# Folding the sinks into the preceding block's rows, with three displaced keys added back by VectorE

## The chip, the cores and the metric

One Trainium2 chip, of which the kernel uses one core. The metric is the device time of one execution in microseconds (us). Executions agree within about 1%; where a run was marked as disturbed (one execution each of two experiments) it is left out of the ratios. The profile is one execution on the same core. A result or run below gives a ratio with its 95% interval; differences under 2% are clear of noise only where that interval leaves out 1. The engines are TensorE (PE), VectorE (DVE), ScalarE (ACT), GpSimd (POOL) and SyncE (SP); SP here only issues DMAs, and GpSimd issues the loads.

## The reference, cut to what matters

```python
# q, k, v: (4, 8, 768, 64) float32; n_sink = 4; window = 128
scores = matmul(q, k.T) / sqrt(64)
keep = (pos < n_sink) | ((rel >= 0) & (rel < window))     # rel = query - key
a = softmax(where(keep, scores, -1e9));  x = matmul(a, v)  # -> (4, 768, 512)
xn = (x - mean) / sqrt(var + 1e-6) * g_ln
out = x + relu(xn @ w_ch1) @ w_ch2                        # 512 -> 2048 -> 512
```

Each query sees the first four keys of its batch (the sinks) and the last 128 keys.

## The kernel before: the parts that matter

There are 24 blocks of 128 queries: block `t` is block `r = t % 6` of batch `b = t // 6`. A block with `r > 0` multiplies its queries with the keys of its own and of the preceding block; from `r = 2` on the sinks are in neither, and get small products of their own. Four blocks make a group, which goes through the two layers of the MLP (`ph` and `pc` in the profile). All instructions come from a planner: a task has a cost, dependencies and a priority, and the planner writes each engine's instructions in the order of its simulated starts. The tiles that matmuls write have names in p: `ps` and `pk` scores, `pv` and `po` products with the values, `pt` and `px` transposes. Fillers are matmuls against the identity, put where the planner expects PE to wait.

```python
def load(fn, land, take=(), desc=1024):               # all q, k, v and weight loads, on GpSimd
    i = plan.add({"POOL": 0.88}, [], fn, (0,), take=take, land=land, after=last_load[0], desc=desc)
...
# sc(): scores of the own and the preceding block go to ps; then, for r >= 2, the sinks' scores:
for h2 in range(2):
    for hp in range(4):
        nc.tensor.matmul(P["pk", t][32 * hp:32 * hp + 32, h2, :], lhsT=ks_of[b][:, h2, hp, :],
                         rhs=qkT[t][:, 0, hp, :], ...)
...
# ACT: exponentials of ps and, apart, of pk (es). av(), for each half of the heads:
if r >= 2:
    for h2 in range(2):
        nc.tensor.matmul(po..., lhsT=ES[t][:, h2, :], rhs=vs_t[b]..., start=(h2 == 0), ...)
for hh in range(4):
    nc.tensor.matmul(po[:, hh, :], lhsT=ee[...0, :], rhs=vn[:, t, h, :], ...)
    if r > 0:
        nc.tensor.matmul(po[:, hh, :], lhsT=ee[...1, :], rhs=vn[:, t - 1, h, :], ...)
...
# from block 8 or so on SP transposes queries and keys by DMA; it also stores the output
nc.sync.dma_start_transpose(qkT[t]..., qn[t]...)
```

What matters of the planner: a dependency fixes a *position in the order of an engine's instructions*. At run time an instruction waits only for data and buffers it really needs.

The softmax here doesn't subtract the row's maximum and nothing guards it: scores larger than these inputs give would overflow.

## Time and profile before

227.5 us, median of 3 runs (227.4 to 227.82).

| | before |
|---|---|
| span of the profiled run | 225.4 us |
| PE busy | 217.0 us (96%) |
| DVE / ACT busy | 135.0 / 104.0 us |
| DMA full until | about 130 us |

PE is the bound, except in the first 26 us, where loads are. The prediction below shows the lines. The first DMA transposes start here (columns: start, length in us, the instruction):

```profile
51.82 5.67 SPq L369 DMA_TRANSPOSE qkT<-qkn  x2
```

### The profile page before, as it was taken

What the parts mean: (1) busy time and instruction counts of PE and PEld (TensorE: products, weight loads), DVE (VectorE), ACT (ScalarE), POOL (GpSimd) and SP (SyncE); (2) the same over time, 40 slices, a digit from 0 to 9 for tenths busy, and PEclk for the clock granted to TensorE, in tenths of its full rate; (3) what the DMA queues carried; (4) which work ended last, traced back from release to release, by engine and by line L of the source; (5) the groups of instructions that cost most, each with busy time, mean ns of one, the idle gap of its engine ahead of it and who ended that gap; (6) DMA issues with size and microseconds to landing.
All of it is one profiled execution on the core that took longest, in us unless ns stands there. A gap on an engine that the chain in (4) does not pass through costs nothing.

```text
span 225.4 us, 4783 instructions
## 1 busy us (share of the span) xinstructions
PE 217.0 (96%) x1921; PEld 121.0 (54%) x1948; DVE 135.0 (60%) x398; ACT 104.0 (46%) x166; POOL 76.0 (34%) x92
## 2 busy tenths in 40 slices
PE   8999999999999999999999999999999999999992
PEld 7766787655455554455555544454555544444440
DVE  5777998779577988863756873654854712100121
ACT  2386788344367731167641258633077600376000
POOL 7994366691695242933088000100000010000000
PEclk9999999999999999999999999999999999999999
DMA  7999999999999999999989994203221021200111
GB/s 43 139 157 206 182 184 209 166 173 192 218 150 129 144 140 189 175 185 191 94 103 158 168 209 88 51 17 102 71 48 23 3 70 47 93 0 3 47 71 69
DMA packets 108709, 26.52 MB, mean 118 GB/s; under 512 B 101520, under 2 KB 105616, under 8 KB 108688
## 3 DMA queue, kind: packets, MB, share of 16 engines
q0 software_dynamic: 79104, 13.64, 81.7%
q1 hardware_dynamic: 29584, 12.59, 30.1%
q8 instruction: 15, 0.25, 0.4%
q14 instruction: 6, 0.05, 0.1%
HBM read 27.27 MB, written 6.29 MB: 149 GB/s over the span
## 4 chain that ended last, share of the span: by engine, by line
PE 81%; DMA 8%; POOL 5%; DVE 3%; issue 1%; ACT 0%; POOLq 0%; ACTq 0%
PE ph L603 34%; PE pc L634 34%; PE ps L406 5%; DMA w1s<-in_moe_w_ch_dram 4%; DMA qkT<-qkn 3%; PE po L501 2%; PE po L504 2%; POOL qkn L267 2%; POOL vn L275 2%; POOL qkn L272 2%; PE po L496 2%; PE pk L413 1%; PE pt L347 1%; DVE xt L517 1%; DVE w1s L299 1%
## 5 line engine op out<-in xcount | busy, mean ns | idle before, releaser
L603 PE MATMUL ph<-xnt,w1s 128*128 128x512 bf16 (+1 forms) x434 | 88.9, 348 | 1.0 <-DVE h L617 0.3
L634 PE MATMUL pc<-w2s,h 128*128 128x512 bf16 x371 | 87.0, 379 | 1.1 <-issue 0.5
L619 ACT ACTIVATE h<-ph 128x512 bf16<-128x512 f32 (+1 forms) x84 | 45.8, 546 | 53.8 <-PE ph L603 52.1
L603 PEld LDWEIGHTS <-w1s 128*128 128x128 bf16 x448 | 41.5, 98 | 35.4 <-ACT h L619 0.5
L634 PEld LDWEIGHTS <-h 128*128 128x128 bf16 x384 | 35.8, 98 | 39.1
L435 ACT ACTIVATE e<-ps 128x1024 bf16<-128x1024 f32 (+1 forms) x48 | 43.7, 951 | 12.5 <-PE ps L406 12.5
L646 DVE SCALAR_TENSOR_TENSOR ot<-pc,rsg,xt 128x512 f32<-128x512 f32 x24 | 17.9, 747 | 38.9 <-PE pc L634 38.9
L548 POOL TENSOR_TENSOR rsg<-ve,eps_half 128x4 f32<-128x4 f32 x6 | 6.2, 1028 | 82.0 <-DVE ve L546 82.0
L267 POOL DMA_DIRECT2D qkn<-in_q_dram x24 | 21.9, 910 | 14.9 <-DMA qkT<-qkn 13.1
L444 DVE TENSOR_TENSOR e<-e,mask_std 128x1024 bf16<-128x1024 bf16 x28 | 18.9, 684 | 10.9 <-ACT e L435 10.9
L617 DVE TENSOR_SCALAR h<-ph 128x512 bf16<-128x512 f32 (+1 forms) x28 | 15.9, 570 | 13.7 <-PE ph L603 13.6
L272 POOL DMA_DIRECT2D qkn<-in_k_dram x24 | 21.7, 903 | 2.8 <-DMA w2s<-in_moe_w_ch_dram 1.4
L275 POOL DMA_DIRECT2D vn<-in_v_dram x24 | 21.8, 912 | 1.8 <-DMA w1s<-in_moe_w_ch_dram 1.8
L517 DVE SCALAR_TENSOR_TENSOR xt<-po,rc 128x256 bf16<-128x256 f32 x48 | 20.4, 425 | 1.7
L501 PE MATMUL po<-vn,e 128*128 128x65 bf16 x192 | 17.1, 193 | 0.1
L537 DVE BATCH_NORM_STATS2 st<-xt 128x6 f32<-128x512 bf16 x24 | 16.4, 684 | 0.0
L406 PEld LDWEIGHTS <-qkT 64*128 64x128 bf16 x352 | 9.9, 94 | 10.4 <-issue 7.8
L406 PE MATMUL ps<-qkT 64*128 64x128 bf16 x352 | 14.7, 218 | 0.7 <-DMA qkT<-qkn 0.4
L482 ACT ACTIVATE es<-pk 128x256 bf16<-128x256 f32 x16 | 6.1, 383 | 19.9 <-PE pk L413 19.8
L514 DVE RECIPROCAL rc<-po 128x4 f32<-128x4 f32 x48 | 8.5, 178 | 11.3 <-PE po L504 10.4
L501 PEld LDWEIGHTS <-e 128*128 128x128 bf16 x192 | 14.0, 97 | 2.1 <-DVE e L444 0.5
L504 PE MATMUL po<-vn,e 128*128 128x65 bf16 x160 | 14.9, 193 | 0.0
(66 smaller groups left out, 146.2 us busy)
## 6 DMA issues: line engine op xcount, KB each, us to landing
out_dram<-ot SPq DMA_DIRECT2D x24, 256.0 KB, 2.5
qkn<-in_q_dram POOLq DMA_DIRECT2D x24, 128.0 KB, 7.1
qkn<-in_k_dram POOLq DMA_DIRECT2D x24, 128.0 KB, 6.8
vn<-in_v_dram POOLq DMA_DIRECT2D x24, 128.0 KB, 7.6
w1s<-in_moe_w_ch_dram POOLq DMA_DIRECT2D x4, 512.0 KB, 10.3
w2s<-in_moe_w_ch_dram POOLq DMA_DIRECT2D x4, 512.0 KB, 10.7
qkT<-qkn SPq DMA_TRANSPOSE x16, 7.2
xnt<-xc SPq DMA_TRANSPOSE x16, 5.6
```

What stands on the lines that cost most here:

```text
L267: nc.gpsimd.dma_start(qn[t][:, 0], q[b, :, rows, :].rearrange("h p d -> p h d"))
L272: nc.gpsimd.dma_start(qn[t][:, 1], k[b, :, rows, :].rearrange("h p d -> p h d"))
L275: nc.gpsimd.dma_start(vn[:, t, :, 0:64], v[b, :, rows, :].rearrange("h p d -> p h d"))
L406: nc.tensor.matmul(ps[:, h2, hh, kb, :], lhsT=qkT[t - kb][rows, 1, hp, :], rhs=qkT[t][rows, 0, hp, :], start=(hh == 0 and kb == 0 and t no ...
L435: nc.scalar.activation(E[t, half][:, :, :, 0:nkb, :], P["ps", t, half][:, :, :, 0:nkb, :], AF.Exp, scale=scale)
L444: nc.vector.tensor_mul(ee[:, :, 0:w], ee[:, :, 0:w], m[:, 0:w].unsqueeze(1).to_broadcast([128, 4, w]))
L501: nc.tensor.matmul(po[:, hh, :], lhsT=ee[:, h % 2, hh // 2, 0, :], rhs=vn[:, t, h, :], start=(r < 2 and hh == 0), stop=(r == 0), skip_grou ...
L504: nc.tensor.matmul(po[:, hh, :], lhsT=ee[:, h % 2, hh // 2, 1, :], rhs=vn[:, t - 1, h, :], start=False, stop=True, skip_group_check=True)
L517: nc.vector.scalar_tensor_tensor(xt[t][:, 256 * half:256 * half + 256].rearrange("p (h d) -> p h d", h=4), in0=po[:, :, 0:64], scalar=1.0, ...
L603: nc.tensor.matmul(ph, lhsT=w1s[:, j, 128 * ht:128 * (ht + 1)], rhs=xnt[g][:, j, cols], start=(j == 0), stop=(j == NDM - 1))
L619: nc.scalar.activation(o, i, AF.Relu)
L634: nc.tensor.matmul(P["pc", t], lhsT=h1[g, ht][:, 128 * ti:128 * (ti + 1)], rhs=w2s[:, ht, :], start=(ht == 0), stop=(ht == NH1 - 1))
```

## The change

The intent: for the eight blocks with `r >= 2` of batches 2 and 3 (14 to 17 and 20 to 23) copy the four sinks over rows 0 to 3 of the preceding block's keys and values. Queries 3 and up of a block do not see those rows anyway, so the sinks need no products of their own. Queries 0, 1 and 2 lose up to three keys that they should see (rows 1 to 3 of the preceding block). Their contribution is computed apart in float32 by DVE, and added to rows 0 to 2 of the result. The inputs of that are fetched by 27 small DMAs. In the same change the planner's model of DMA landing times is altered, two buffer rings shrink, and the variance may run on ACT.

```diff
+    def corrections(dep):
+        for i in range(3):
+            def fetch(e, i=i):
+                for b in range(1, B):
+                    at = slice(12 * i + 4 * (b - 1), 12 * i + 4 * b)          # four partitions
+                    nc.sync.dma_start(fq[at], q[b, :, 256:768, :].rearrange("h (r x) d -> x r h d", x=128)[i])
+                    for to, src in ((fk, k), (fv, v)):
+                        nc.sync.dma_start(to[at].rearrange("r h p d -> r h (p d)"),
+                                          src[b, :, 129:641, :].rearrange("h (r x) d -> r h x d", x=128)[:, :, 0:3, :]
+                                          .rearrange("r h x d -> r h (x d)"))
+            fetched.append(plan.add({"SP": 4.0}, [dep], fetch, (0, 7, i), land=.7, lag=2.0, ...))
         ... fourteen DVE operations on 36 partitions, one ACT exponential -> fc ...
+        def spread(e):
+            for i in range(3):
+                nc.sync.dma_start(fcb[i:i + 1], fc[12 * i:12 * i + 12])
 ... in block(t), with fold = r >= 2 and t >= FOLD (12):
+        if fold:
+            nc.vector.tensor_copy(qkT[t - 1][:, 1, :, 0:4], kss_of[b])        # sinks' keys
+            nc.vector.tensor_copy(vn[0:4, t - 1], vn[0:4, t - r])             # sinks' values
-        sink = r >= 2 and halves[-1] == 1
+        sink = r >= 2 and not fold and halves[-1] == 1
-                if r >= 2:
+                if sinks:                                                     # r >= 2 and not fold
                     ... the sinks' products in po ...
+                if fold:
+                    nc.vector.tensor_add(po[0:3], po[0:3], fcb[:, t - RB - 2 * b, 4 * half:4 * half + 4, :])
 ... and elsewhere:
-    RINGS = dict(... ks=2, vs=2, ... xn=4, h1=32, ot=4)
+    RINGS = dict(... ks=2, kss=2, vs=2, ... xn=2, h1=20, ot=4)
-        v_ = d_var[t] = plan.add({"DVE": .87}, ...)
+        v_ = d_var[t] = plan.add({"DVE": .87, "ACT": .95}, ...)               # ACT: Square with accum_out
+    corrections(quanta[FDEP])                                                 # FDEP = 32, a piece of the MLP
 ... cut: the planner's landing(), a lag for each load, masks, counts of readers
```

More of the change, by code (lines that the diff above doesn't have):

```diff
@@ L47, in run @@
         ends = {}
-        dma_free = free["DMA"]
+        dma = {"POOL": free["DMA"], "SP": free["DMA"]}
         order = []
@@ L94, in run @@
             if t["land"] is not None:
-                dma_free = max(dma_free, start + 1.5) + t["land"]
-                end = dma_free + (0.6 if t["lag"] is None else t["lag"])
+                at = self.landing(dma, e, start, t["land"])
+                end = at + (0.6 if t["lag"] is None else t["lag"])
                 if t["desc"]:
-                    queued.append((dma_free, t["desc"]))
+                    queued.append((at, t["desc"]))
             done[i] = (e if t["land"] is None else None, start + cost, end)
@@ L112, in run, with landing @@
         return order
+    @staticmethod
+    def landing(dma, e, start, land):
+        if e == "POOL":
+            dma["POOL"] = max(dma["POOL"], start + 1.5) + land
+        else:
+            begin = max(dma["SP"], start + 1.5)
+            dma["SP"] = begin + land + min(land, max(0.0, dma["POOL"] - begin))
+            dma["POOL"] = max(dma["POOL"], begin) + land
+        return dma[e]
     @staticmethod
@@ L165 @@
     LDN, QKN = 4, 5
-    RINGS = dict(pa=4, ps=2, ld=LDN, qk=QKN, ks=2, vs=2, e=8, es=3, xc=4, xn=4, h1=32, ot=4)
+    RINGS = dict(pa=4, ps=2, ld=LDN, qk=QKN, ks=2, kss=2, vs=2, e=8, es=3, xc=4, xn=2, h1=20, ot=4)
     plan = Planner(RINGS)
@@ L206 @@
     ks_t = [consts.tile([128, 2, 4, 32], BF16, name=f"ks_{i}") for i in range(2)]
+    junk = consts.tile([128, DM], BF16, name="junk")
+    kss = [consts.tile([128, 4, 4], BF16, name=f"kss_{i}") for i in range(2)]
+    mask_c = consts.tile([36, 1, 3], FP32, name="mask_c")
+    tmp_c = consts.tile([36, 1, 3], FP32, name="tmp_c")
+    iota_c = consts.tile([36, 3], I32, name="iota_c")
+    fq = consts.tile([36, H, 64], FP32, name="fq")
+    fk = consts.tile([36, H, 3, 64], FP32, name="fk")
+    fv = consts.tile([36, H, 3, 64], FP32, name="fv")
+    fs = consts.tile([36, H, 3], FP32, name="fs")
+    fe = consts.tile([36, H, 3], FP32, name="fe")
+    fc = consts.tile([36, H, 65], FP32, name="fc")
+    fcb = consts.tile([3, 12, H, 65], FP32, name="fcb")
     xt = [consts.tile([128, DM], BF16, name=f"xt_{t}") for t in range(NT)]
@@ L221, in make_masks @@
         nc.gpsimd.iota(iota_h, pattern=[[-32, 4]], base=0, channel_multiplier=1)
+        nc.gpsimd.iota(iota_c, pattern=[[12, 3]], base=12, channel_multiplier=-1)
         v_.tensor_scalar(ident, iota_d, 0.0, None, op0=ALU.is_equal)
@@ L251 @@
     last_load = [None]
+    n_load = [0]
     def load(fn, land, take=(), desc=1024):
-        i = plan.add({"POOL": 0.88}, [], fn, (0,), take=take, land=land, after=last_load[0], desc=desc)
+        n = n_load[0]
+        n_load[0] += 1
+        i = plan.add({"POOL": 1.4 if n == 0 else 0.9}, [], fn, (0,), take=take, land=land, after=last_load[0], desc=desc,
+                     lag=.9 if n < 8 else 2.4 if n < 42 else 1.2)
         last_load[0] = i
@@ L313 @@
     P = {}
+    folds = []
     def w0(e, s):
@@ L324, in opening, with mask, step @@
         D["mc"] = plan.add({"DVE": 1.3}, [d_q[0]], make_masks_c, (0, 1, 5))
+    def corrections(dep):
+        fetched = []
+        for i in range(3):
[7 more added lines that the diff above has]
+                                          .rearrange("r h x d -> r h (x d)"))
+            fetched.append(plan.add({"SP": 4.0}, [dep], fetch, (0, 7, i), land=.7, lag=2.0,
+                                    after=fetched[-1] if fetched else None))
+        def mask(e):
+            nc.vector.tensor_scalar(mask_c[:, 0, :], iota_c, 0.0, None, op0=ALU.is_gt)
+        def step(cost, deps, fn, eng="DVE"):
+            return plan.add({eng: cost}, deps, fn, (0, 7, 8))
+        d = step(.2, fetched, mask)
+        for p in range(3):
+            d = step(.65, [d], lambda e, p=p: nc.vector.tensor_mul(fk[:, :, p, :], fk[:, :, p, :], fq))
+            d = step(.65, [d], lambda e, p=p: nc.vector.tensor_reduce(
+                fs[:, :, p:p + 1], fk[:, :, p:p + 1, :], axis=mybir.AxisListType.X, op=ALU.add))
+        d = step(.3, [d], lambda e: nc.scalar.activation(fe, fs, AF.Exp, scale=scale), "ACT")
+        d = step(.2, [d], lambda e: nc.vector.tensor_mul(fe, fe, mask_c.to_broadcast([36, H, 3])))
+        for p in range(3):
+            d = step(.65, [d], lambda e, p=p: nc.vector.tensor_mul(
+                fv[:, :, p, :], fv[:, :, p, :], fe[:, :, p:p + 1].to_broadcast([36, H, 64])))
+        d = step(.2, [d], lambda e: nc.vector.tensor_reduce(fc[:, :, 64:65], fe.unsqueeze(2),
+                                                            axis=mybir.AxisListType.X, op=ALU.add))
+        d = step(.65, [d], lambda e: nc.vector.tensor_add(fv[:, :, 0, :], fv[:, :, 0, :], fv[:, :, 1, :]))
+        d = step(.65, [d], lambda e: nc.vector.tensor_add(fc[:, :, 0:64], fv[:, :, 0, :], fv[:, :, 2, :]))
+        def spread(e):
+            for i in range(3):
+                nc.sync.dma_start(fcb[i:i + 1], fc[12 * i:12 * i + 12])
+        done = plan.add({"SP": 1.4}, [d], spread, (0, 7, 9), land=.2, lag=2.0)
+        for i in folds:
+            plan.tasks[i]["deps"].append(done)
@@ L335, in block @@
         split = t in SPLIT
+        fold = r >= 2 and t >= FOLD
         def tr(a):
@@ L356, in block @@
         n_s = lambda u: 2 if u in SPLIT_S else 1
-        qk_readers = n_s(t) + (0 if last else n_s(t + 1)) + (1 if r == 0 else 0)
+        qk_readers = n_s(t) + (0 if last else n_s(t + 1)) + (sum(any((u >= FOLD) == w for u in range(t + 2, t + RB)) for w in (0, 1)) if r == 0 else 0)
         if split:
@@ L416, in sc, with fold_k, fold_v @@
             return f
+        if fold:
+            def fold_k(e):
+                nc.vector.tensor_copy(qkT[t - 1][:, 1, :, 0:4], kss_of[b])
+            def fold_v(e):
+                nc.vector.tensor_copy(vn[0:4, t - 1], vn[0:4, t - r])
+            kf = plan.add({"DVE": .13}, [d_s[t - 1], d_kss[b]], fold_k, (0, t, 1), drop=[("kss", b)])
+            vf = plan.add({"DVE": .25}, d_a[t - 1] + [d_v[t - r]], fold_v, (0, t, 1))
         s_ = []
@@ L420, in block @@
             cost = .22 * nkb + .43 * nkb * (t in MPE)
-            sink = r >= 2 and halves[-1] == 1
+            sink = r >= 2 and not fold and halves[-1] == 1
             x_ = plan.add({"PE": cost * len(halves) / 2 + .15 + SINK * sink},
                           d_c[t] + (d_c[t - 1] if r else []) + ([D["mb"]] if t in MPE and r else [])
-                          + ([d_ks[b]] if sink else []), sc(halves),
+                          + ([d_ks[b]] if sink else []) + ([kf] if fold else []), sc(halves),
                           (0, t, 2), take=[("ps", ("ps", t, h), 1) for h in halves]
@@ L440, in mk @@
             def mk(e, half=half):
-                m = (mask_zero, mask_one)[r] if r < 2 else mask_std
+                m = mask_zero if r == 0 else mask_one if r == 1 or fold else mask_std
                 w = 128 * nkb
@@ L446, in block, with mkf @@
             ms.append(x_ if t in MPE else plan.add({"DVE": .68 if r else .4}, [x_], mk, (0, t, 4)))
-        if r == 0:
+        blocks = [u for u in range(t + 2, t + RB)] if r == 0 else []
+        old = [u for u in blocks if u < FOLD]
+        new = [u for u in blocks if u >= FOLD]
+        if new:
+            def mkf(e, s):
+                kss_of[b] = kss[s]
+                nc.vector.tensor_copy(kss[s], qkT[t][:, 1, :, 0:4])
+            d_kss[b] = plan.add({"DVE": .13}, d_c[t], mkf, (0, t + 2, 0), take=[("kss", ("kss", b), len(new))],
+                                drop=[("qk", t)])
+        if old:
             def mks(e, s):
@@ L454, in mks @@
                     nc.vector.tensor_copy(ks_of[b][rows, h2], qkT[t][rows, 1, :, 0:32])
-            d_ks[b] = plan.add({"DVE": .3}, d_c[t], mks, (0, t + 2, 0), take=[("ks", ("ks", b), 4)],
+            d_ks[b] = plan.add({"DVE": .3}, d_c[t], mks, (0, t + 2, 0), take=[("ks", ("ks", b), len(old))],
                                drop=[("qk", t)])
@@ L468, in block @@
                 pv = plan.add({"PE": .13}, [d_v[t], D["mc"], s_[0]] + vs_d, pv_, (0, t + 2, 0),
-                              take=[("pa", ("pv", b, half), 1)] + ([("vs", ("vs", b), 8)] if half == 0 else []))
+                              take=[("pa", ("pv", b, half), 1)] + ([("vs", ("vs", b), 2 * len(old))] if half == 0 else []))
                 def vs_(e, half=half, hs=hs):
@@ L477, in block @@
             d_vs[b] = vs_d
-        a_deps = [d_v[t]] + ([d_v[t - 1]] if r else [])
-        if r >= 2:
+        a_deps = [d_v[t]] + ([d_v[t - 1]] if r else []) + ([vf] if fold else [])
+        sinks = r >= 2 and not fold
+        if sinks:
             def es_(e):
@@ L493, in av @@
                 ee = E[t, half]
-                if r >= 2:
+                if sinks:
                     for h2 in range(2):
@@ L501, in av @@
                     nc.tensor.matmul(po[:, hh, :], lhsT=ee[:, h % 2, hh // 2, 0, :], rhs=vn[:, t, h, :],
-                                     start=(r < 2 and hh == 0), stop=(r == 0), skip_group_check=True)
+                                     start=(not sinks and hh == 0), stop=(r == 0), skip_group_check=True)
                     if r > 0:
@@ L505, in av @@
                                          start=False, stop=True, skip_group_check=True)
-            a = plan.add({"PE": (.12, .25, .37)[min(r, 2)]}, a_deps + [ms[half]], av, (0, t, 5),
+            a = plan.add({"PE": .12 if r == 0 else .37 if sinks else .25}, a_deps + [ms[half]], av, (0, t, 5),
                          take=[("pa", ("po", t, half), 1)],
-                         drop=[("e", t, half)] + ([("es", t), ("vs", b)] if r >= 2 else []))
+                         drop=[("e", t, half)] + ([("es", t), ("vs", b)] if sinks else []))
+            d_a.setdefault(t, []).append(a)
             def nm(e, half=half):
                 po = P["po", t, half]
+                if fold:
+                    nc.vector.tensor_add(po[0:3], po[0:3], fcb[:, t - RB - 2 * b, 4 * half:4 * half + 4, :])
                 rc = small.tile([128, 4], FP32, name="rc")
@@ L520, in nm @@
                     accum_out=sums[t][:, half:half + 1])
-            ns.append(plan.add({"DVE": .60}, [a], nm, (0, t, 6), drop=[("po", t, half)]))
+            if fold:
+                folds.append(len(plan.tasks))
+            ns.append(plan.add({"DVE": .93 if fold else .60}, [a], nm, (0, t, 6), drop=[("po", t, half)]))
         def ln(e, s):
@@ L535, in st @@
                 mvg[g] = small.tile([128, 4, 2], FP32, name="mvg")
-            st_ = small.tile([128, 6], FP32, name="st")
-            nc.vector.bn_stats(st_, xt[t])
-            nc.vector.bn_aggr(mvg[g][:, ti, :], st_)
-        v_ = d_var[t] = plan.add({"DVE": .87}, [l_] + ([d_var[t - 1]] if ti else []), st, (0, t + 6, 7))
+            if e == "DVE":
+                st_ = small.tile([128, 6], FP32, name="st")
+                nc.vector.bn_stats(st_, xt[t])
+                nc.vector.bn_aggr(mvg[g][:, ti, :], st_)
+            else:
+                root = 1.0 / float(DM) ** 0.5
+                st_ = small.tile([128, 1], FP32, name="nb")
+                nc.scalar.mul(st_, sums[t][:, 2:3], -root)
+                nc.scalar.activation(junk, xt[t], AF.Square, bias=st_, scale=root, accum_out=mvg[g][:, ti, 1:2])
+        v_ = d_var[t] = plan.add({"DVE": .87, "ACT": .95}, [l_] + ([d_var[t - 1]] if ti else []), st, (0, t + 6, 7))
         if ti == len(GROUPS[g]) - 1:
@@ L582 @@
     quanta = []
-    ks_of = {}
+    ks_of, kss_of, d_kss, d_a = {}, {}, {}, {}
     h1 = {}
@@ L668 @@
     W2AT = 6
+    FOLD = 12
+    FDEP = 32
     SEQ = [x for g in range(NG) for x in ((1, g), (2, g))]
```

## The prediction

> **What bounds the kernel now.** I read the page first, then the busy time of each engine by stretch, then TensorE's timeline around one late attention block, then the chain of waits in the opening. One core, so there is no die to compare, and the granted clock is full.
>
> The page: busy time, the chain that ended last by engine, and the DMA row of the 40 slices.
>
> ```profile
> PE 217.0 (96%) x1921; PEld 121.0 (54%) x1948; DVE 135.0 (60%) x398; ACT 104.0 (46%) x166; POOL 76.0 (34%) x92
> ...
> DMA  7999999999999999999989994203221021200111
> ...
> PE 81%; DMA 8%; POOL 5%; DVE 3%; issue 1%; ACT 0%; POOLq 0%; ACTq 0%
> ```
>
> TensorE (PE) carries four fifths of the chain. What is not PE is DMA and GpSimd's issuing of loads, and the DMA row says when: the engines are full from the first slices to about 130 us and nearly empty after it.
>
> Busy time in four stretches (columns: PE, its weight loads, DVE, ACT, GpSimd; then clock, DMA share, GB/s):
>
> ```profile
> 0.00:27.00 27.00, 25.27 (x339) 19.31 (x340) 20.16 (x77) 15.43 (x24) 20.18 (x29) 1.00 1.53 145
> 27.00:60.00 33.00, 32.25 (x353) 21.95 (x355) 27.78 (x82) 18.07 (x34) 18.75 (x22) 1.00 1.87 180
> 60.00:180.00 120.00, 118.44 (x1054) 61.28 (x1069) 80.68 (x231) 60.45 (x92) 36.04 (x41) 1.00 1.20 120
> 180.00:222.00 42.00, 41.05 (x188) 18.48 (x189) 6.34 (x11) 10.01 (x17) 1.01 (x1) 1.00 0.13 47
> ```
>
> From 60 us on PE is busy 118.4 of 120 us while DVE is at two thirds and ACT at half: PE work removed there should come off the end one for one. The first stretch differs: part of PE's 25.3 busy us are warming matmuls against the identity that the schedule puts where it expects PE to wait. After the 34 on zeros there are 66 of them (the rows of that one line count 37 + 13 + 11 + 5), about 56 ns apart.
>
> One late block, from PE's timeline (start, length, then the instruction):
>
> ```profile
> 163.60 0.62 PE L406 MATMUL ps<-qkT 64*128 64x128 bf16 x16
> 164.15 0.29 PE L413 MATMUL pk<-qkT,ks 128*32 128x128 bf16 x8
> 164.38 2.76 PE L603 MATMUL ph<-xnt,w1s 128*128 128x512 bf16 x11
> 166.98 0.28 PE L496 MATMUL po<-vs,es 128*128 128x130 bf16 x2
> 167.10 0.19 PE L501 MATMUL po<-vn,e 128*128 128x65 bf16 x1
> ```
>
> Read starts, not lengths, because matmuls overlap: the eight sink scores (pk) occupy PE from 164.15 to 164.38, 0.23 us, and the two sink products of one half (po from vs, es) from 166.98 to 167.10, 0.12 us.
>
> The chain of waits in the opening:
>
> ```profile
> 12.34 0.70 POOL w1s L290
> 13.04 9.37 DMA w1s<-in_moe_w_ch_dram
> 22.41 0.02 issue
> 22.43 0.62 DVE w1s L299 x2
> 23.05 0.33 DVE h L617
> ...
> 26.52 2.78 PE ph L603 x24
> ```
>
> Until 26.5 us the end is set by loads: attention inputs of four blocks, then the first-layer weights. A weight chunk takes 9.4 us because it queues behind the loads before it.
>
> **What the Trainium skill says.** (1) "TensorE: Matmul & The Clock Gate", section "Step-by-step: what each phase is for", gives a back-to-back gap of N/2.4 + 2.5 ns: 216 ns at 512 columns and about 57 ns at 130. The trace agrees: starts of the 512-column matmuls have a median spacing of 216 ns, those of 130 columns 59 ns. (2) "ScalarE: Activation LUTs", section "What ACT_TABLE_LOAD costs": a table load is about 1283 ns, and an ACTIVATE with a pointer bias takes about 280 ns + 0.833 ns per element. The trace has one load of 1283 ns in all; its 128x512 activation with a pointer scale takes 717 ns, the formula gives 707. (3) "DMA: Bandwidth & Descriptors", section "Why a DMA increments its semaphore by 16 and not by 1": the number of DMA engines used divides the slowest dimension on both sides, and on the SyncE path the lowest-numbered ones are taken. A fetch of four rows would then use four engines. No view here shows engines, so this stays an inference. (4) Same page, "Queues, rings and completion order": a DMA engine takes packets in turn from the queue rows that have work. The trace has no competing queue in the opening except the 2 KB gain load.
>
> **The change, part by part.** Blocks 14-17 and 20-23, eight of them, lose the separate sink path.
>
> PE removed. Per block 0.23 (pk) + 2 x 0.12 (po) = 0.47 us; times 8 is 3.7 us. Batches 2 and 3 also lose the four pv products; two of these start at 12.11 with the next work at 12.23, so 0.12 us each, 0.5 us. Together 4.2 us, all in stretches where PE is the bound. This is the gain.
>
> PE added. The order of the changed kernel has 83 identity fillers where there were 66, 22 instead of 18 before the first transpose: 17 x 0.056 = 0.95 us. Where PE would have waited anyway they cost nothing; the four at the start may cost 0.2 us.
>
> ACT. Eight sink exponentials of 383 ns go (-3.1 us). Fifteen of the 24 variances move here: each a small multiply (I take 0.25 us) and a 128x512 square with pointer bias (0.71 us): +14.4 us. The changed program still has one table load. About 115 us of 225: not the bound.
>
> DVE. Removed: 15 statistics pairs at 684 + 182 ns = 13.0 us, 4 key copies at 320 ns and 4 vs products at 424 ns = 3.0 us. Added: 16 corrections of 3x260 in PSUM; a 260-element product from PSUM takes 424 ns, so 6.8 us; eight copies of four key columns and eight of 4x520 values, some 0.15 and 0.3 us, 3.6 us; the one-off correction sums, eleven operations on 512 float32 elements at about 0.65 us (the 128x512 TENSOR_SCALAR takes 685 ns) and three small ones, 7.7 us. Net about +2 us in 225; not the bound. New waits exist (keys of block t wait for the scores of t-1, values for its products), but those lie several us earlier on PE at this spacing, so I count 0 to 0.5 us. The correction is 0.42 us per half before a PSUM bank is freed; pk and pv bank uses fall away in return.
>
> DMA. Twenty-seven fetches of four partitions each and three spreads go on SyncE's queue. The intent is that they run after the first layer of group 0, but that is a position in the schedule only. In the built order 18 of them stand right behind the gain load and ahead of the first output store, and they wait for nothing but earlier fetches (8 may be in flight). So they start at 1 us, inside the opening. SyncE's gain load took 0.45 us to issue; 18 at that rate last to about 9 us. Size: 6 of 4x8 rows of 256 B and 12 of 4x8 rows of 768 B. If each uses four engines, every one of the four gets 6x8x256 + 12x8x768 = 86 KB. A w1s chunk reads 1 MB in about 2.6 us on 16 engines, some 25 KB per us per engine: an estimate of 3.4 us of extra work on four of the engines. About 1 us of this falls into DMA's idle time before 3 us and near 4.7 us; the rest delays the loads and the weights, since a load is not complete until its last engine is. Against it stands slack: fillers in the opening, and about 1.3 us of PE gaps at 20 to 27 us that the new order should avoid. I take +1.5 us for the opening.
>
> Planning. The landing model is changed and buffer counts shrink (xn 4 to 2, h1 32 to 20). A group's first-layer outputs need 16 of 20, so four are spare while the last group drains: no wait expected. Before, one PE gap of 0.6 us at 58.9 us waited for the transposed block 8; the new model should place it better.
>
> Sum: 227.5 - 4.2 + 1.5 + 0.2 = 225.0 us.
>
> **Rivals.** A, the fetches cost nothing: the fillers stand for waiting anyhow, and the better landing model closes some gaps. Then 227.5 - 4.2 = 223.3, or 222.5 with 0.8 us of recovered gaps: just over 2% faster. For it: PE has slack in the opening; the fetches add only 2% to 26.5 MB. Against: the DMA row is full from 4 us on. B, the opening loses the full 3 us and DVE, which is 8.5 of 10 us busy at 50-60 and 70-90 us, delays masks and bank releases during the one-off sums: 227 us, nothing gained. For it: the chain of waits goes through the weight DMA to 22.4 us. Against: DVE sheds statistics in the same stretch. C, the serial fold chain (scores, key copy, scores; products, value copy, products) becomes a wait per block: 8 x 0.5 us would also return the gain. The spacing of blocks, some 8 us, speaks against it.
>
> **Range and chances.** The gain term is firm to 0.3 us; the opening runs from -0.8 to +3, the rest from 0 to +0.8. So 222.8 to 227.0 should hold it 8 times in 10. Two per cent faster means below 223.0, which needs rival A: 0.17. Slower by 2% needs several of the losses and more: 0.02.
>
> **What would show it.** Right: PE busy falls by about 4 us; es and pk rows halve; between 60 us and the end the time shortens by about 4 us; the first dense first-layer work (26.5 us before) begins 1 to 2 us later, with landings of the first loads and w1s lengthened. Wrong: the opening ends no later (rival A), or PE gains gaps before ps or po of folded blocks whose releaser is a DVE copy (rival C), or around 55 to 75 us with the fk, fv sums as releaser (B).

## The result, and the profile after

The changed kernel takes 233.56 us, median of 4 runs (232.52 to 234.52), against 227.45 us (227.35 to 227.82) for the kernel before. The ratio is 1.0265 with a 95% interval of 1.0219 to 1.0311. A ratio here is the mean time of one kernel's fast runs over that of the other's of the same rounds, so it is not quite the ratio of the medians that are quoted. The prediction was wrong: 225.0 us and a range of 222.8 to 227.0. The page of the profiled run (span 231.9 us):

```profile
PE 215.1 (93%) x1841; PEld 119.4 (51%) x1865; DVE 138.7 (60%) x412; ACT 114.3 (49%) x200; POOL 76.1 (33%) x93
...
PE 81%; DMA 13%; POOL 2%; issue 1%; DVE 0%; ACT 0%; POOLq 0%
```

There are 80 PE instructions fewer, about as planned (100 removed, 17 fillers added), but the span grew by 6.5 us while PE's busy time fell by 1.9: PE has 8.4 us more in which it does nothing. The chain's DMA share went from 8% to 13%. Busy time in the two stretches that lost, of the four shown before (PE, its weight loads, DVE, ACT, GpSimd; then clock, DMA share, GB/s):

```profile
0.00:27.00 27.00, 19.79 (x257) 15.06 (x257) 12.49 (x55) 8.52 (x12) 18.65 (x28) 0.94 1.74 138
...
60.00:180.00 120.00, 115.17 (x970) 58.32 (x984) 87.00 (x247) 67.58 (x120) 36.42 (x41) 1.00 1.40 130
```

In the opening PE is busy 19.8 us where it was 25.3; from 60 us on 115.2 of 120 us where it was 118.4, although there is less to do. The opening's clock of 0.94 is an average. The trace has it at full speed but for 19.0 to 22.5 us, where it is half (0.51 on average; the fourth of the slices below, of 5.8 us each, has it). In the kernel before every slice is 9. The page's row after the change:

```profile
PEclk9997999999999999999999999999999999999998
```

That is up to 1.7 us of PE work lost (an estimate, 3.4 us at half speed), on top of the waits. Which waits PE has in all, by line and releaser (us, times, longest):

```profile
PE pt L425 <- DMA qkn<-in_k_dram: 4.3, 2, 2.4
PE ps L484 <- DMA qkT<-qkn: 3.6, 2, 2.6
PE pt L425 <- DMA qkn<-in_q_dram: 1.9, 1, 1.9
```

The first and third are the loads of queries and keys in the opening; the second is the DMA transposes later. No DVE copy holds PE. In the opening PE's timeline reads so (the brackets give the idle time before the group, and the releaser):

```profile
9.57 0.40 PE L425 MATMUL pt<-ident,qkn 128*128 128x128 bf16 x4 [2.35 <-DMA qkn<-in_k_dram]
...
16.63 0.40 PE L425 MATMUL pt<-ident,qkn 128*128 128x128 bf16 x4 [1.85 <-DMA qkn<-in_q_dram]
18.98 0.58 PE L425 MATMUL pt<-ident,qkn 128*128 128x128 bf16 x4 [1.96 <-DMA qkn<-in_k_dram]
```

In the kernel before, the same transposes stood at 7.37 and 12.23 us with no wait:

```profile
7.37 0.39 PE L347 MATMUL pt<-ident,qkn 128*128 128x128 bf16 x4
...
12.23 0.61 PE L347 MATMUL pt<-ident,qkn 128*128 128x128 bf16 x8
```

So the loads come later, and what differs is how long they take to land. Issues in the first 14 us of the kernel before, then of the changed one (last column: median us from issue to landing):

```profile
qkn<-in_q_dram POOLq DMA_DIRECT2D x4, 128.0 KB, 4.1
qkn<-in_k_dram POOLq DMA_DIRECT2D x4, 128.0 KB, 4.2
vn<-in_v_dram POOLq DMA_DIRECT2D x4, 128.0 KB, 5.0
```

```profile
qkn<-in_q_dram POOLq DMA_DIRECT2D x4, 128.0 KB, 8.4
qkn<-in_k_dram POOLq DMA_DIRECT2D x4, 128.0 KB, 8.9
vn<-in_v_dram POOLq DMA_DIRECT2D x4, 128.0 KB, 11.4
```

GpSimd issued these loads at the same times in both kernels, within 0.2 us; the landing times have doubled. That feeds back: GpSimd waits for landings before it issues more. Its first-layer weight chunks, in the kernel before (first line) and in the changed one:

```profile
12.25 3.07 POOL L290 DMA_DIRECT2D w1s<-in_moe_w_ch_dram  x4
...
16.86 0.74 POOL L318 DMA_DIRECT2D w1s<-in_moe_w_ch_dram  x1 [3.58 <-DMA qkn<-in_q_dram]
19.22 1.57 POOL L318 DMA_DIRECT2D w1s<-in_moe_w_ch_dram  x2 [1.61 <-DMA qkn<-in_k_dram]
```

The last chunk's issue starts at 20.0 us; in the kernel before all four were issued in one go from 12.25 us, the last at 14.5, without a wait. And SP's queue in the changed kernel says what is new in that stretch:

```profile
1.26 0.44 SPq L365 DMA_DIRECT2D fq<-in_q_dram  x1
...
10.04 0.31 SPq L367 DMA_DIRECT2D fv<-in_v_dram  x1
53.52 0.38 SPq L764 DMA_DIRECT2D out_dram<-ot  x1
...
59.62 0.25 SPq L367 DMA_DIRECT2D fv<-in_v_dram  x1
...
61.85 5.67 SPq L447 DMA_TRANSPOSE qkT<-qkn  x2
...
75.59 2.54 SPq L397 DMA_DIRECT2D fcb<-fc  x3
...
81.62 6.62 SPq L447 DMA_TRANSPOSE qkT<-qkn  x2
```

Read it in three parts. Eighteen fetches run at 1.3 to 10.3 us. The other nine stand behind the first output store, at 54 to 60 us, and the transposes wait behind them: they start at 61.85, not at 51.82. At 75.6 us the three spreads stand ahead of transposes too. The chain of waits picks up both sets of transposes:

```profile
61.85 8.71 DMA qkT<-qkn
...
81.62 10.19 DMA qkT<-qkn
```

The intended gain is there as well. A folded block on PE:

```profile
147.16 0.62 PE L484 MATMUL ps<-qkT 64*128 64x128 bf16 x16
147.71 2.77 PE L714 MATMUL ph<-xnt,w1s 128*128 128x512 bf16 x11
```

After the 16 scores the MLP goes on at once (0.55 us from start to start): no pk stands between them.

To see where time goes, I took the start of the n-th weight load of the MLP in two profiled runs and subtracted; both runs have the same number of them (448 and 384 rows for the two layers). It is one run of each, so a few tenths mean nothing. Changed minus before: +6.9 us at 30 us, +10.7 at 86 us, then falling, as folded blocks pass, to +6.8 at 177 us and the end. So the loss is made before 90 us and the fold gives 3.9 us back. PE's busy time fell by only 1.9 us and not by the 4 that the prediction looked for; at half clock matmuls follow one another more slowly (the products with the values start 0.06 us apart at 20 us, 0.03 in the kernel before). In runs 10 and 9 below, without such a stretch, it is 213.1 and 212.8 us where it was 217.0.

### The profile page after: what moved, and what is told of

Its sections match the earlier page's. It is cut to its first block, busy times and chain, and to the rows that moved or that the text cites. A ratio compares the mean times of both kernels' runs of the same rounds, so it can differ in the third digit from the quotient of the medians.

```text
span 231.9 us, 4716 instructions
## 1 busy us (share of the span) xinstructions
PE 215.1 (93%) x1841; PEld 119.4 (51%) x1865; DVE 138.7 (60%) x412; ACT 114.3 (49%) x200; POOL 76.1 (33%) x93
## 4 chain that ended last, share of the span: by engine, by line
PE 81%; DMA 13%; POOL 2%; issue 1%; DVE 0%; ACT 0%; POOLq 0%
PE ph L714 33%; PE pc L745 33%; DMA qkT<-qkn 8%; DMA qkn<-in_k_dram 5%; PE ps L484 5%; PE po L601 2%; PE po L604 2%; PE pt L425 1%; POOL qkn L295 1%; PE ps L475 1%; PE px L670 1%; POOL qkn L300 1%; PE po L596 1%; PE pk L491 1%; PE po L195 1%
## 5 line engine op out<-in xcount | busy, mean ns | idle before, releaser
L730 ACT ACTIVATE h<-ph 128x512 bf16<-128x512 f32 (+1 forms) x81 | 44.6, 552 | 40.8 <-PE ph L714 40.0
L300 POOL DMA_DIRECT2D qkn<-in_k_dram x24 | 21.6, 901 | 2.6 <-DMA w2s<-in_moe_w_ch_dram 1.5
L728 DVE TENSOR_SCALAR h<-ph 128x512 bf16<-128x512 f32 (+1 forms) x31 | 16.9, 556 | 8.5 <-PE ph L714 8.3
L533 DVE TENSOR_TENSOR e<-e,mask_one 128x1024 bf16<-128x1024 bf16 x22 | 14.6, 686 | 4.9 <-ACT e L524 4.9
L601 PE MATMUL po<-vn,e 128*128 128x65 bf16 x192 | 17.4, 196 | 0.0
L601 PEld LDWEIGHTS <-e 128*128 128x128 bf16 x192 | 14.6, 99 | 3.7 <-DVE e L533 0.3
L604 PE MATMUL po<-vn,e 128*128 128x65 bf16 x160 | 15.4, 196 | 0.0
L648 ACT ACTIVATE nb<-sums 128x1 f32<-128x1 f32 x15 | 3.0, 203 | 21.2 <-DVE sums L631 21.2
L604 PEld LDWEIGHTS <-e 128*128 128x128 bf16 x160 | 11.5, 99 | 2.5
```

Source lines behind the costliest of these rows:

```text
L300: nc.gpsimd.dma_start(qn[t][:, 1], k[b, :, rows, :].rearrange("h p d -> p h d"))
L601: nc.tensor.matmul(po[:, hh, :], lhsT=ee[:, h % 2, hh // 2, 0, :], rhs=vn[:, t, h, :], start=(not sinks and hh == 0), stop=(r == 0), skip_ ...
L604: nc.tensor.matmul(po[:, hh, :], lhsT=ee[:, h % 2, hh // 2, 1, :], rhs=vn[:, t - 1, h, :], start=False, stop=True, skip_group_check=True)
L730: nc.scalar.activation(o, i, AF.Relu)
```

## The experiments

The theory after reading: the fetches cost the time, because each touches four partitions only, and so loads a few DMA engines heavily while each load of queries and keys needs all of them. Rivals: (a) the fetches are harmless, and the new plan (landing model, lags, rings, ACT variances) is worse; (b) it is their bytes or their number that cost, not their width; (c) the sums on DVE and the spreads cost it; (d) folding does not gain what the removed matmuls promise.

The test of correctness needs a word first. Three experiments below leave the correction out or feed it zeros, and all three still passed as correct: three queries of 128 in a third of the blocks, one to three keys of some 130 each, disappear in the tolerance. "Correct" therefore proves nothing about the corrections.

**Run 1: no fetches.** The changed kernel; DVE zeroes the three tiles instead.

```diff
-                for b in range(1, B):
-                    ... nine fetches ...
+                if i == 0:
+                    for z in (fq, fk, fv):
+                        nc.vector.memset(z, 0.0)
```

> The changed kernel with the 27 fetches replaced by three memsets of zeros (wrong result on purpose: the three queries lose their displaced keys). Everything else, the order of the other engines included, is kept. Theory T1 (the fetches in the opening cost the 7 us there, and the nine later ones the waits near 69 and 89 us): 223 to 224 us, no PE gap over 1 us in the opening. Rival R1 (the new plan, its fillers and its landing model cost the opening): stays above 230 us. If the opening is mended but the waits near 69 and 89 us stay: 226 to 227 us.

Measured: 227.68 us against 227.79, ratio 1.0002 (0.9953 to 1.0052). The loss is gone, but not all of the gain appeared. The edit was flawed; DVE's timeline:

```profile
41.82 0.48 DVE L365 MEMSET fq<- 36x512 f32 x1
42.58 1.34 DVE L365 MEMSET fk<- 36x1536 f32 x1 [0.27 <-issue]
44.18 1.34 DVE L365 MEMSET fv<- 36x1536 f32 x1 [0.27 <-issue]
```

Nearly four microseconds of zeroing ahead of attention's work held PE for 3.1 us, from 44.7 to 47.8 us, and from 48.1 to 51.5 us the clock was half. The expected 223 to 224 us was missed. Run 5 repeats it without that.

**Run 2: the kernel before with the 18 early fetches, results unused.**

```diff
         nc.sync.dma_start(gt, moe_g_ln.rearrange("(j p) -> p j", p=128))
+        for n_ in range(6):
+            b_, i_ = 1 + n_ % 3, n_ // 3
+            at = slice(12 * i_ + 4 * (b_ - 1), 12 * i_ + 4 * b_)
+            nc.sync.dma_start(fq[at], ...)          # as in the change: 4 partitions x 8 rows
+            for to, src in ((fk, k), (fv, v)):
+                nc.sync.dma_start(to[at]..., ...)
```

> The kernel before, with the same 18 fetches into tiles that nobody reads, right behind the gain load. T1: +6 to +8 us over before, so 233 to 236 us, with PE gaps of about 2 us each before transposes of blocks 0 to 2. R1: within 1 us of before, 227 to 228.5 us.

Measured: 231.82 us against 227.79, ratio 1.0179 (1.0142 to 1.0215). Nothing waits for these fetches, and they cost 4 us, less than the 6 to 8 expected. Its opening looks like that of the changed kernel, PE busy 21.1 of 27 us:

```profile
0.00:27.00 27.00, 21.07 (x275) 14.95 (x275) 15.17 (x58) 11.37 (x16) 19.45 (x28) 0.94 1.71 146
```

The clock is half from 18.2 to 21.6 us here too. Rival (a) cannot explain this run.

**Run 3: as many rows and bytes, on 16 partitions.**

```diff
-            nc.sync.dma_start(fq[at], ...)                  # 4 partitions x 8 rows
+                rows_ = src[b_].rearrange("h (r x) d -> (h r) (x d)", r=4)[:, 64 * n_:64 * n_ + 64 * w_]
+                nc.sync.dma_start(to[:, n_], rows_.rearrange("(a c) d -> a c d", c=2))   # 16 x 2 rows
```

> As e2, but each dead fetch has 16 partitions of two rows, so the same 32 rows and bytes could be spread over 16 DMA engines instead of four. If it is the concentration on four engines that costs: 228 to 230 us. If it is the count of bytes or rows or of DMAs: as e2_dead4, 233 to 236 us.

Measured: 227.18 us against 227.79, ratio 0.9983 (0.9959 to 1.0007): free, and below the expected 228 to 230. The loads land nearly as in the kernel before:

```profile
qkn<-in_q_dram POOLq DMA_DIRECT2D x4, 128.0 KB, 4.4
qkn<-in_k_dram POOLq DMA_DIRECT2D x4, 128.0 KB, 5.1
vn<-in_v_dram POOLq DMA_DIRECT2D x4, 128.0 KB, 6.1
```

Bytes and number are those of run 2, so rival (b) falls, but for two things. SP took 0.59 us to issue each fetch here and about 0.3 in run 2, so the burst was also slower (run 12 takes this up). And the rows are read from other addresses of q, k and v than in run 2, which no run tests apart.

**Run 4: the changed kernel with its fetches later.** Nine steps of three, each tied to a piece of the MLP's schedule, behind the first output store.

```diff
-        for i in range(3):
+        for n_ in range(9):
...
-            fetched.append(plan.add({"SP": 4.0}, [dep], ...))
+            fetched.append(plan.add({"SP": 1.0}, [dep[n_]], ...))
-    corrections(quanta[FDEP])
+    corrections([quanta[FDEP + FSTEP * n] for n in range(9)])     # 38, 41, ...
```

> The changed kernel with the fetches in nine steps of three, placed in the plan so that all stand behind the first output store on SyncE's queue, between transposes and stores. Right result. T1: the opening is as before (first dense first-layer work at 26 to 27 us); 223.5 to 226 us depending on what the fetches do to the transposes between 50 and 90 us. R1: above 230 us.

Measured: 232.15 us against 227.79, ratio 1.02 (1.0171 to 1.0229; one run of four was disturbed and is left out). The opening mended (PE busy 24.8 of 27 us), and the loss came back later, so that the expected 223.5 to 226 us was missed:

```profile
60.00:120.00 60.00, 51.73 (x440) 26.91 (x446) 43.56 (x116) 30.68 (x52) 24.21 (x28) 0.97 2.24 148
```

PE lacks 8.3 us of 60 there; in the whole run it waits four times for DMA transposes, 7.5 us in all, and the clock is half from 79.3 to 82.7 us. In SP's queue the transposes stand behind fetches, and two fetches (at 71.5 and 79.8 us) had waited 2.2 and 4.2 us until earlier transposes had landed, by SP's waits. Moving narrow DMAs out of the opening is not enough when they share a queue with transposes.

**Run 5: no fetches, cleanly.** As run 1, but ACT writes the zeros in the first 6 us, where it is idle.

```diff
+        for z, n in ((fq, 512), (fk, 1536), (fv, 1536)):
+            nc.scalar.copy(z_, zeros[0:36, 0:1].to_broadcast([36, n]))    # z_: z with its free dims flat
...
-                for b in range(1, B):
-                    ... nine fetches ...
+                pass
```

> e1 again without its flaw: the three memsets of e1 ran on DVE from 41.8 to 45.5 us and held PE for 3.1 us. Here ACT, idle then, writes the zeros in the first 6 us. No fetch, wrong result for three queries per block on purpose. Theory T1 (fetches alone cost the opening): 223 to 224.5 us, with one PE gap of about 1.6 us left near 82 us. Rival R1 (the new plan costs as much as the fold saves): 227 us or more.

Measured: 224.97 us against 228.14, ratio 0.9874 (0.9839 to 0.9908), half a microsecond above the expected range. Against the changed kernel's 1.0265 this is the price of the fetches: 1.0265/0.9874 is 1.040, some 9 us. By the n-th weight load the changed kernel lies behind this one by 7.1 to 7.5 us from 20 to 50 us (the 18 early fetches), and by 9.1 from 87 us on (with the nine late ones, another 2.0). One wait of PE is left:

```profile
PE ps L481 <- DMA qkT<-qkn: 2.0, 1, 2.0
```

It comes at 80.8 to 82.8 us. The transposes start at 73.1 us on SP, behind the three spreads (66.3 to 68.8) and a transpose of the MLP's input; how much of the wait the spreads make is not shown.

**Run 6: a repair.** Three fetches of 24 partitions in place of 27 of four, right behind the gain load; 221 KB in place of 516, since each key and value is fetched once and not for each query. The sums are rewritten for that layout, and start at a later piece of the MLP.

```diff
+    def fetch_all():
+        for to, src, first in ((fq, q, 256), (fk, k, 129), (fv, v, 129)):
+            nc.sync.dma_start(to..., src.rearrange("b h s d -> (b h) s d")[H:B * H, first:first + 512, :]
+                              .rearrange("p (r x) d -> p r x d", x=128)[:, :, 0:3, :]...)   # 24 partitions
...
-    FDEP = 32
+    FDEP = 64
```

> A repair, meant to give the full result: the displaced keys, values and queries of three batches in three fetches of 24 partitions (12 DMA engines if the number divides 24, each key fetched once, 221 KB instead of 516 KB), still right behind the gain load; the sums planned after the first layer of group 1. If the number of engines and bytes is what counts: opening as before, 222.5 to 224.5 us. If any fetch in the opening costs: 226 us or more.

Measured: 230.74 us against 228.14, ratio 1.0116 (1.0072 to 1.016). A miss, and not by the fetches: the opening is as before (PE busy 25.5 of 27 us). SP and PE's wait tell the rest:

```profile
89.00 2.63 SPq L393 DMA_DIRECT2D fcb<-fc  x3
91.74 1.29 SPq L672 DMA_TRANSPOSE xnt<-xc  x1
```

```profile
PE ph L710 <- DMA xnt<-xc: 5.6, 1, 5.6
```

The sums ran as one chain on DVE from 79.6 to 88.9 us, in front of attention's work; the spreads waited for them on SP, and the transposes of the MLP's input behind the spreads. PE then waited 5.6 us for its input, and the clock was half from 97.1 to 104.0 us, of which 3.1 us after the wait. Rival (c) is a real cost, if a smaller one in the changed kernel.

**Run 7: run 6 with the planner as before** (landing model, lags, variances on DVE only; a revert of those hunks).

> e6 with the schedule model of before (landing times, lags, variances on DVE alone; the smaller rings stay). If the new model helps: 1 us or more slower than e6. If it is neutral: within 1 us of e6. If the new model is what makes the waits at 70 to 90 us: faster than e6.

Measured: 228.76 us against 228.14, ratio 1.002 (0.9972 to 1.0067; one run of four disturbed and left out). Two microseconds faster than run 6, the outcome that the expectation had named for "the new model makes the waits". It is not the whole of it: a PE wait of the same kind stays, 2.4 us at 97.5 us. In run 8 and run 9 the new model costs nothing, so the order matters only together with where the sums stand.

**Run 8: the changed kernel with no folding and no corrections.** What is left is the new plan.

```diff
-    FOLD = 12
+    FOLD = 24
-    corrections(quanta[FDEP])
```

> The changed kernel with nothing folded and no corrections: new schedule model, smaller rings and variances on ACT alone. T1: within 1 us of before (226.5 to 228.5 us). R1: 230 us or more.

Measured: 228.4 us against 228.14, ratio 1.0013 (0.9969 to 1.0058). The plan, the shorter rings and the ACT variances together neither cost nor gain more than about 1 us. Rival (a) is out as the cause of the 6 us; run 5, which keeps the changed kernel's order, says the same.

**Run 9: the repair, with the sums spread out.** Each operation of the sums is tied to every second piece of the MLP, and the spreads follow three pieces after the last.

```diff
+        at = [FDEP]
         def step(cost, deps, fn, eng="DVE"):
-            return plan.add({eng: cost}, deps, fn, (0, 7, 8))
+            at[0] += 2
+            return plan.add({eng: cost}, deps + [quanta[at[0]]], fn, (0, 7, 8))
-        done = plan.add({"SP": 1.4}, [d], spread, (0, 7, 9), land=.2, lag=2.0)
+        done = plan.add({"SP": 1.4}, [d, quanta[at[0] + 3]], spread, (0, 7, 9), land=.2, lag=2.0)
-    FDEP = 64
+    FDEP = 44
```

> e6 with every step of the sums tied to a later piece of MLP work (one step for two pieces, from piece 46 on) and the spreads three pieces after the last. Full result. e6 lost 5.7 us at 95 us, where PE waited for the transposed xnt of group 3. Theory T2 (the sums as one serial run of 9 us on DVE, ahead of attention work, and the spreads in the way of the transposes on SyncE's queue make that wait): 222.5 to 225 us with no PE gap over 1.5 us after 27 us. Rival (the schedule model's placing of the transposes makes it): the gap stays, 227 us or more.

Measured: 223.22 us, median of 6 (221.81 to 224.18), against 227.84: ratio 0.9811 (0.9771 to 0.985). This is the whole computation, with corrections, and faster than both kernels (by 1.9%, so the 2% verdict is "unclear", but the interval leaves out 1). The expectation was met: no PE wait over 0.4 us after 27 us. The test does not see the corrections. From the edit, key row p of the three goes to queries 0 to p, as it should. Its busy time in two stretches:

```profile
0.00:27.00 27.00, 24.92 (x358) 19.50 (x359) 20.60 (x77) 15.23 (x25) 20.23 (x29) 1.00 1.57 154
...
60.00:180.00 120.00, 118.07 (x956) 59.28 (x971) 86.79 (x251) 67.69 (x117) 35.53 (x40) 1.00 1.26 122
```

PE is busy as in the kernel before in both, and has the fold's work less to do.

**Run 10: the fold alone.** The changed kernel without fetches, sums, spreads and the additions to po; its result lacks the displaced keys.

```diff
-                if fold:
-                    nc.vector.tensor_add(po[0:3], po[0:3], fcb[...])
-    corrections(quanta[FDEP])
```

> The changed kernel with the fold alone: no fetches, sums, spreads or corrections added (wrong result for three queries per block on purpose). This is the gain term by itself: 4.2 us of PE work, so 222.5 to 224 us if PE is the bound throughout and the waits near 55 and 80 us come from the sums and spreads. If those waits are the schedule's own: 224.5 to 226 us.

Measured: 223.03 us, median of 6, against 227.84: ratio 0.9807 (0.9775 to 0.9839), 4.4 us. The gain is as large as the removed matmuls promise, so rival (d) is out. Run 9 equals it within the intervals, so well-placed corrections cost at most about 1 us (0.6 us by the last weight loads of the two profiles).

**Run 11: the 18 dead fetches on 8 partitions x 4 rows**, an edit like run 3's.

> As e3_dead16 with 8 partitions of four rows in each of the 18 dead fetches: the same rows and bytes. If the share of work on the busiest DMA engine sets the delay: between e3 (nothing) and e2 (4 us), about 1 us over before, 227.5 to 229.5 us. If the shape of the destination doesn't matter: 226.5 to 227.5 us as e3.

Measured: 228.23 us against 227.84, ratio 1.0029 (0.9996 to 1.0062). Between runs 2 and 3, and much nearer to 3: 1.8%, 0.3% and -0.2% for 4, 8 and 16 partitions, of which the last two cannot be told from nothing. The time lies in the expected range, and the loads land as in run 3 (4.6, 5.1 and 6.0 us for q, k and v; in run 2, 7.1, 7.6 and 9.6). SP issued these at 0.67 us each, slower still than in run 3, so pace and width remained mixed.

**Run 12: the 18 dead fetches of run 2, paced.** A 4 KB load over 16 partitions after each one.

```diff
+    pad = consts.tile([16, 18, 64], FP32, name="pad")
+    def pause():
+        nc.sync.dma_start(pad[:, n_], v[0].rearrange("h (r x) d -> (h r) (x d)", r=2)[:, 64 * n_:64 * n_ + 64])
...
             nc.sync.dma_start(fq[at], ...)
+            pause()
             for to, src in ((fk, k), (fv, v)):
                 nc.sync.dma_start(to[at]..., ...)
+                pause()
```

> The kernel before with the 18 fetches of four partitions, as in the first dead-fetch run, but after each one a pad load of 16 partitions x 256 B (4 KB), so that SyncE issues the fetches about as slowly as it issued those of 16 partitions (0.6 us each) and of 8 (0.67 us). If it is the fetches' width that costs, pacing changes little: ratio 1.013 to 1.022, and the loads of the first 14 us take 6 to 8 us to land. If the pace alone made the wide fetches cheap, the ratio falls to 0.998 to 1.006 with landings of 4.4 to 5.5 us. Between these: both have a part.

Measured: 231.35 us against 227.74, ratio 1.0154 (1.0119 to 1.0188). The first four-partition fetches now follow one another at 0.7 us and the last is issued at 21 us, a slower burst than in run 3 or 11, and the cost stays. In the first 14 us the loads land so:

```profile
qkn<-in_q_dram POOLq DMA_DIRECT2D x4, 128.0 KB, 6.0
qkn<-in_k_dram POOLq DMA_DIRECT2D x4, 128.0 KB, 6.4
vn<-in_v_dram POOLq DMA_DIRECT2D x4, 128.0 KB, 7.8
```

Pacing eases it a little and no more, as the expectation for width said. The pads add 74 KB over 16 partitions, where run 3 moved over four times that on 16 partitions for nothing; they double the number of DMAs, which no run tests apart. So it is the width of the fetches and not their pace.

## Why the prediction was wrong, by its own steps

**The step that failed is "+1.5 us for the opening".** The prediction saw that 18 fetches run inside the opening, and why, and it named four engines. Then it sized the damage too small, in these ways. First, the delay of the loads: 3.4 us of extra work less 1 us of idle time makes 2.4, and the loads of the first 14 us landed 4.3, 4.7 and 6.4 us later (q, k, v). Whether the 3.4 us itself was too small, or what came of it, the traces do not tell. SyncE's queue at 3 to 19 us in the changed kernel and then in run 3 (packets, MB, share of 16 engines' time):

```profile
q1 hardware_dynamic: 592, 0.32, 12.7%
...
q1 hardware_dynamic: 817, 0.34, 11.0%
```

The first share is 0.127 x 16 x 16 = 32.5 us of packets, 8.1 us for each of four engines if there were four. But packet times overlap (those of the loads' own queue add up to 212% in that stretch), so this is an upper estimate, and the free fetches of run 3 take nearly as much. Second, it took the delay of the loads for the whole damage and missed the feedback on GpSimd: the last weight chunk is issued 5.5 us later (20.0 against 14.5). Third, it let filler matmuls and PE gaps absorb part of the delay; PE waited 6.2 us for loads at 7 to 19 us all the same, after the fillers were used up. Fourth, it had no term for the clock, and 3.4 us after these waits ran at half. Half clock also came with waits of 2.0 to 5.6 us in runs 1, 2, 4, 6 and 7, but not with a wait of 2.0 us in run 5; what sets it was not tested. Measured with the order of the plan unchanged, run 5 against the changed kernel, the early fetches cost about 7.1 us in place of 1.5.

**"The rest from 0 to +0.8" failed too.** The order of SP's queue was not in the sum at all. The nine late fetches put the transposes off, which goes with 2.0 us (9.1 less 7.1). The sums and spreads cost another 1.7 us: run 5 gains 2.3 us at the last weight loads, run 9, with the same corrections and better placed, 4.0. Altogether -4.0 + 1.7 + 7.1 + 2.0 = +6.8 us, which is the shift of the last weight loads; the terms are differences of the same measure, so that they add up is bookkeeping (one profile each, with tenths of noise), and runs 2 to 5 and 10 are the evidence.

**The gain of 4.2 us was right.** Run 10 measures 4.4 us and run 9, by weight loads, 4.0. It also comes where it was predicted, from the first folded blocks to the end. One line is misread in the working: a single pv product, not two, starts at 12.11 us, so 0.12 us each is right.

**The costs on DVE and ACT were sized well.** The moved variances and the corrections:

```profile
L649 ACT ACTIVATE junk<-xt,nb 128x512 bf16<-128x512 bf16 x15 | 10.8, 722 | 0.5
L615 DVE TENSOR_TENSOR po<-po,fcb 3x260 f32<-3x260 f32 x16 | 6.7, 421 | 0.6
...
L649 ACT ACTIVATION_READ_ACCUMULATOR junk<-xt,nb 128x1 f32 x15 | 2.8, 186 | 0.0
```

The 0.71 us of the prediction for the square became 722 ns, and the 424 ns for a correction became 421. The third row, reading the accumulator out, was not in the sum; ACT is not the bound, and run 10, which has these too, keeps the full gain. DVE grew by 3.7 us where the sum had about 2. "Not the bound" was right for DVE's total and misleading for its order: run 6 shows 9 us of correction work, placed as one block, taking 5.6 us from PE.

**The rivals.** A (free fetches) is what fetches on 16 partitions do in run 3, not these. B (opening loses 3 us, one-off sums disturb) named both mechanisms and had each too small or too vague. C (a wait per folded block) did not occur: PE's waits have no DVE copy among their releasers, and run 10 keeps the full gain. "The new model should place it better" did not show: run 8 is at 1.0013.

**What stays open.** No view shows which DMA engines a transfer used. That narrow fetches cost and wide ones do not is shown by runs 2, 3, 11 and 12; the third point that the prediction cites from the Trainium skill ("DMA: Bandwidth & Descriptors", section "Why a DMA increments its semaphore by 16 and not by 1") says how the number of engines follows from the shape. That four busy engines hold up every load is inferred from it; it fits but is not shown, and few engines are not told apart from few partitions at the destination. The dead fetches cost 4 us in the order of the kernel before (by weight loads 5.2 us at 30 us, 4.7 at the end) and the early ones 7.1 us in that of the changed kernel; the last weight chunk was issued at 18.2 us in the former and at 20.0 in the latter, which goes the right way. But it isn't all: in run 12 that issue comes at 15.5 us, one microsecond late only, and the run still loses 3.6 us; there the fetches go on to 21 us, beside the weights themselves. How the loss divides between late issue and slow landing was not tested.

## What to carry to other kernels

A dependency that only places an instruction in a schedule is not a wait: see where such a DMA lands in the issuing engine's order, and what it then runs beside. Side fetches next to a saturated load stream should use many partitions (16 here; fewer DMAs were not tested apart), and one-off work, on VectorE or in SyncE's queue, should be dealt out between the bound engine's pieces and not stand in one block ahead of what feeds it. Look at the clock row as well: a wait of the bound engine can be followed by a slow stretch. And ask whether the test would notice if the delicate part were missing.

## What the Trainium skill lacked or had wrong

- "DMA: Bandwidth & Descriptors" says how many engines a transfer uses but not what a narrow one costs beside full-width loads. Here 18 fetches with 0.34 MB in all cost 1.8% on 4 partitions (1.5% when paced), 0.3% on 8 and -0.2% on 16, and doubled the landing time of 128 KB loads from 4.1 to 8.4 us in the changed kernel.
- The same page, section "Anatomy of one DMA — SWDGE (gpsimd) path", calls descriptor generation "small, variable" for DMAs that GpSimd issues; I found no figure by width for SyncE on this chip. There the issue of 32 rows took about 0.3 us on 4 partitions, 0.67 on 8 and 0.59 on 16, and that of 16 rows on 16 partitions 0.32 us, enough to set the pace of a burst.
- "ScalarE: Activation LUTs" has no cost for reading the accumulator out: 186 ns after each of 15 ACTIVATEs of 128x512. Its duration for the ACTIVATE itself held (722 ns measured, 707 by its formula).
